# Dense sums computed in PV's 64x32 tiles, on both sides of PV, in a fused attention and gated-MLP kernel

## The chip, the core and the metric

The kernel runs on one core of a Trainium2 chip. A core has one TensorE (PE) for matrix products, three elementwise engines, VectorE (DVE), ScalarE (ACT) and GpSimd (POOL), and SyncE (SP), which here only starts DMA transfers. Each engine works through a queue of its own, strictly in the order in which the program wrote its instructions, and waits at semaphores for what other engines or transfers must deliver. Products are summed in PSUM, eight banks of 128 x 512 float32. The metric is the device time of one execution in microseconds (us).

## The reference

With x of 2048 x 640 (S x D), 32 heads of 20 and a hidden width of 1536:

```python
xn = layernorm(x)                                  # over 640
q, k, v = split(xn @ wqkv)                         # 32 heads, Dh = 20
scores = q k^T * Dh**-0.5, kept where 0 <= i - j < 256
A = softmax(scores) v, heads joined, @ wo
B = (sigmoid(xn @ w_gate) * (xn @ w_up)) @ w_down
out = x + A + B
```

All inputs and the output are bfloat16.

## The kernel before, in words

**Chunks.** The 2048 rows are worked on in four chunks c of 512. For each chunk there are projections to q, k and v, a gate and an up product for each of 12 blocks f of 128 hidden units, attention, and an output stage of four row blocks. Activations lie transposed, as `xnT[c]` (128 x 5 x 512).

**Dense sums.** A "dense sum" is one accumulation of full 128x128 matmuls into one PSUM bank: `pqk` (L330, five matmuls of 512 columns, one for each of five blocks m of q and of k), `pv` (L360, five of 320 columns, for four row blocks s and two halves), `pg` and `pu` (L450, L457, five of 512 columns each), and `y` (12 of 320 columns at L471 over `ht` and `wd`, then five at L478 over `oc` and `wo`; two halves for each row block s). Each is read afterwards by one or two instructions: `st` (L334 on DVE for q, L336 on ACT for k), which SP stores to a scratch in memory; the casts of `pv` into `v` (L369, on DVE for the first half and on ACT for the second); a tanh `th` of `pg` on ACT (L453); `h`, which multiplies `th` and `pu`, on DVE (L461); and `rows` (L482, DVE).

**Attention.** Heads are handled four at a time (a group), two groups at a time (a "head pair" of groups o and o + 1, PSUM accumulators `acc`). The sliding window is cut into squares of 64 x 64, and the squares of a head pair are packed into "score runs" of 128 x 4 x 512 scores: 15 runs for chunk 0 and 20 for each later one, five for each head pair, 75 in all, numbered from 0 in the order of the loop at L754. In a run `scores` (L519) issues matmuls in tiles of 20x64 (20 of the array's rows, 64 of its columns; L526), eight of which work side by side, into `ps`, which takes four PSUM banks; there is one such buffer. One exp on ACT (L531) turns it into a P tile `pT`; POOL then zeroes what the window excludes (`affine_select`, L538). Some steps ("late") get one more mask on DVE (L543, "the edge step"); in chunks 1 to 3 it is the last of a head pair's five runs.

**PV.** When all runs of a head pair are there, `pv` (L545) multiplies P with V in tiles of 64x32 (L557), again eight side by side, into two `acc` banks: 96 matmuls for a head pair. `finish_group` transposes each `acc` on DVE (L569) and puts the scaling (`scale_group`: reciprocal L577, multiplications L581, transpose L585) on the list `fill.behind`, of which one entry goes out with each later piece of dense work, two if `hurry` is set.

**PSUM.** `ps` holds four banks, the pool `ps_d` the other four. Dense sums and the `acc` banks share `ps_d`; a new tile takes the bank that has been free for longest, and its first matmul waits until that bank's last reader is done.

**The order of the work.** The program's order is written by hand. The loop at L754 goes over the 75 runs. If `due` has a head pair at step t, its PV goes out first (run t is then the first run of the next head pair), then run t's scores, and then dense work out of `Fill`: generators that issue a dense sum and yield its cost in ns. `pull` (L623) draws from the front generator until the given ns are used up; `one` (L604) draws once. A step draws 1800 ns (`APART`) and a `credit` that spreads what must be done by a deadline over the steps up to it; a "late" step draws 1000 of it before its edge step. `mix` (L632) puts pieces of a second generator between those of a first: the layer norm of the next chunk (`g_norms`: statistics, then four `xn` on DVE, L291, stored by SP; `g_turns`: transposes to `xnT`, L313), and gate and up sums between v and output sums. The generators in order: gate and up sums of chunk 0, then, for each later chunk, its q and k sums (`g_qk`), its v sums (`g_v`, mixed with gate and up), the rest of its gate and up, and the output of the chunk before it (`g_out`). `shut` holds an output stage back until the last PV of its chunk.

**Q and K.** The stores of `st` are read back by `spread` (L340) into `qT` and `kT` tiles of two head pairs (128 x 4 x 512), from pools `qp` (3) and `kp` (5). A zeroed tile of the `kT` pool clears the padding of the scratch at the start (L194).

Of the kernel before, what the change touches and what calls it, by code (L numbers as in the profile page):

```python
# [9 lines left out]
P = 128  # L10
S = 2048
D = 640
H = 32
DH = 20
F = 1536
DC = D // P
FC = F // P
CW = 512
NCH = S // CW
SBC = CW // P  # L20
HG = 4
NG = H // HG
GH = NG // 2
VW = DH + 1
VH = 16 * VW + 11
HALF = 320
# [12 lines left out]
BF16 = mybir.dt.bfloat16  # L39
FP32 = mybir.dt.float32  # L40
# [6 lines left out]
U = 64  # L47
PTW = 10 * U
# [64 lines left out]
def kernel(  # L113
# [11 lines left out]
    nc = tc.nc  # L125
# [4 lines left out]
    def pool(name, bufs, **kw):  # L130
        return ctx.enter_context(tc.tile_pool(name=name, bufs=bufs, **kw))
# [3 lines left out]
    lnp = pool("lnp", 4)  # L135
    xtp = pool("xtp", 2)
    stp = pool("stp", 6)
    qp = pool("qp", 3)
    kp = pool("kp", 5)
    vp = pool("vp", 10)  # L140
    hp = pool("hp", 15)
    pp = pool("pp", 5)
    op = pool("op", 7)
    onp = pool("onp", 2)
    tp = pool("tp", 2)
# [19 lines left out]
    wd = const.tile([P, FC, D], BF16, name="wd")  # L165
# [24 lines left out]

    scratch = {w: tc.dram_tile([H * 32, CW], BF16, name=f"s{w}") for w in "qk"}
    xn_rows = [tc.dram_tile([CW, D], BF16, name=f"xr{k}") for k in range(2)]
    zero = kp.tile([P, GH, CW], BF16, name="kT")
    nc.gpsimd.memset(zero[:, 0:3, :], 0.0)  # L194

    def clear(w):
        rows = scratch[w].rearrange("(h j) s -> h (j s)", j=32)[:, DH * CW:]
        nc.sync.dma_start(out=rows.rearrange("h (a e) -> h a e", a=4), in_=zero[:, 0:3, :])

    def load_gu(t, w, k, lo=0, hi=FS):  # L200
        nc.sync.dma_start(out=t[k][:, :, lo:hi],
# [118 lines left out]
    qk = {}  # L320
    vt = {}

    def proj_block(w, c, m):


        base = 0 if w == "q" else D
        ps = ps_d.tile([P, CW], FP32, name="pqk", tag="d")
        for d in range(DC):
            wt = wqkv[:, d, base:base + D].rearrange("p (k m) -> p m k", m=DC)
            nc.tensor.matmul(ps, lhsT=wt[:, m, :], rhs=xnT[c][:, d, :],  # L330
                             start=(d == 0), stop=(d == DC - 1))
        st = stp.tile([P, CW], BF16, name="st")
        if w == "q":
            nc.vector.tensor_copy(out=st, in_=ps)  # L334
        else:
            nc.scalar.copy(out=st, in_=ps)  # L336
        dst = scratch[w].rearrange("(h j) s -> h j s", j=32)
        nc.sync.dma_start(out=dst[:, 4 * m:4 * m + 4, :], in_=st)

    def spread(w, c, g0, g1):  # L340

        half, first = divmod(g0, GH)
        if first == 0:
            qk[w, c, half] = (qp if w == "q" else kp).tile([P, GH, CW], BF16, name=w + "T")
        src = scratch[w].rearrange("(a b p) s -> b p a s", a=2, p=P)
        for b in range(g0 // 2, g1 // 2):
            o = 2 * b - half * GH
            nc.sync.dma_start(out=qk[w, c, half][:, o:o + 2, :], in_=src[b])

    def new_v(c, s):  # L350
        v = vp.tile([P, 2, VH], BF16, name="v")
# [1 line left out]
        nc.gpsimd.memset(v[:, :, 0:16 * VW].rearrange("p k (h d) -> p k h d", d=VW)[:, :, :, DH:VW], 0.5)  # L353
        nc.gpsimd.memset(v[:, :, 16 * VW:], 0.0)

    def project_v(c, s, hf, lo=0, hi=DC, ps=None):
        if ps is None:
            ps = ps_d.tile([P, CW], FP32, name="pv", tag="d")
        for d in range(lo, hi):
            nc.tensor.matmul(ps[:, 0:HALF], lhsT=xnT[c][:, d, s * P:(s + 1) * P],  # L360
                             rhs=wqkv[:, d, 2 * D + hf * HALF:2 * D + (hf + 1) * HALF],
                             start=(d == 0), stop=(d == DC - 1))
        return ps

    def copy_v(c, s, hf, ps, copy, us=(0, 1)):

# [5 lines left out]
    def proj_v(c, s, hf, copy):  # L372
        copy_v(c, s, hf, project_v(c, s, hf), copy)
# [29 lines left out]
            yield 0  # L403

    def g_qk(c):
        for w in "qk":
            for m in range(DC):
                proj_block(w, c, m)
                if c == 0 and w == "q" and m == 1:
                    load_x(1)  # L410
                if c == 0 and w == "q" and m == 3:
                    load_gu(wu, B_w_up, 0, FS // 2)
                if c and w == "k" and m == 1:
                    spread("q", c, 0, GH)
                yield 5 * MM
        if c == 0:
            spread("q", c, 0, 2)
            spread("k", c, 0, 2)
            spread("q", c, 2, 4)
            spread("k", c, 2, 4)  # L420

    def g_v(c):
        for s in range(SBC):
            new_v(c, s)
            for hf in range(2):
                proj_v(c, s, hf, nc.scalar.copy if hf else nc.vector.tensor_copy)
                if hf == 0:
                    yield 5 * 136
            if s == 0:
                spread("k", c, 0, 2)  # L430
                spread("k", c, 2, GH)
            if c == 1 and s == 1:
                load_wo()
            if s == (2 if c == 1 else 1):
                spread("q", c, GH, NG)
                spread("k", c, GH, NG)
            yield 5 * 136


    ht = {}  # L440
# [1 line left out]
    def part(w, d, f):  # L442
        k, first = divmod(f * P, FS)
        return w[k][:, d, first:first + P]

    def g_gu(c, f0, f1):
        for f in range(f0, f1):
            pg = ps_d.tile([P, CW], FP32, name="pg", tag="d")
            for d in range(DC):
                nc.tensor.matmul(pg, lhsT=part(wg, d, f), rhs=xnT[c][:, d, :],  # L450
                                 start=(d == 0), stop=(d == DC - 1))
            th = tp.tile([P, CW], FP32, name="th")
            nc.scalar.activation(out=th, in_=pg, func=TANH, scale=0.5)  # L453
            yield 5 * MM
            pu = ps_d.tile([P, CW], FP32, name="pu", tag="d")
            for d in range(DC):
                nc.tensor.matmul(pu, lhsT=part(wu, d, f), rhs=xnT[c][:, d, :],  # L457
                                 start=(d == 0), stop=(d == DC - 1))
            h = hp.tile([P, CW], BF16, name="h")
            ht[c, f] = h  # L460
            nc.vector.scalar_tensor_tensor(out=h, in0=th, scalar=1.0, in1=pu, op0=ADD, op1=MULT)  # L461
            yield 5 * MM


    oc = {}
# [7 lines left out]
            if f % 6 == 5:  # L473
                yield 6 * 136

    def add_wo(c, s, y, cut):
        for m in range(DC):
            nc.tensor.matmul(y[:, 0:cut[1] - cut[0]], lhsT=oc[c, m][:, s * P:(s + 1) * P],  # L478
                             rhs=wo[:, m, cut[0]:cut[1]], start=False, stop=(m == DC - 1))

    def add_x(y, cut, rows):
        nc.vector.scalar_tensor_tensor(  # L482
# [9 lines left out]
        sb = c * SBC + s  # L492
        queue.dma_start(out=out2[sb * P:(sb + 1) * P, cut[0]:cut[1]], in_=rows[:, cut[0]:cut[1]])

    def outp(c, s, ys, rows):
        for y, cut in zip(ys, HALVES):
            add_wo(c, s, y, cut)
        for y, cut in zip(ys, HALVES):
            add_x(y, cut, rows)
        store(c, s, rows)  # L500

    def g_out(c, between, ahead=()):
        nxt = new_rows(c, 0)
        for s in range(SBC):
            rows = nxt
            if s == 0:
                yield from ahead
            if s + 1 < SBC:
                nxt = new_rows(c, s + 1)
            ys = [ps_d.tile([P, CW], FP32, name=f"y{i}", tag="d") for i in range(2)]  # L510
            for y, cut in zip(ys, HALVES):
                yield from down(c, s, y, cut)
            if s == 0:
                yield from between
            outp(c, s, ys, rows)
            yield 10 * 136


    def scores(c, step):  # L519
        pt = pp.tile([P, HG, PTW], BF16, name="pT")  # L520
        ps = ps_s.tile([P, HG, CW], FP32, name="ps")
        for o, j, q, n, col in sorted(step["pieces"], key=lambda x: -x[3]):
            kc, kb = divmod(c * CW // U + j, CW // U)
            for a in range(2):
                for i in range(HG):
                    nc.tensor.matmul(  # L526
                        ps[a * U:(a + 1) * U, i, col * U:(col + n) * U],
                        lhsT=qk["k", kc, o // GH][32 * i:32 * i + DH, o % GH + a, kb * U:(kb + 1) * U],
                        rhs=qk["q", c, o // GH][32 * i:32 * i + DH, o % GH + a, q * U:(q + n) * U],
                        start=True, stop=True)  # L530
        nc.scalar.activation(out=pt[:, :, 0:CW], in_=ps, func=EXP, scale=SCALE)  # L531
        for diag, u, n in step["masks"]:
# [217 lines left out]
    fill.pull(6 * 5 * MM)  # L750
    parts = {}
    credit = 0
    fill.shut = {"out0", "out1", "out2"}
    for t, (c, k, step) in enumerate(todo):  # L754
        if k == 0 and c > 0:
            fill.until(f"qk{c}")
        if k == 2 and c > 0:
            fill.until(f"v{c}")
        if t in due:
            fill.flush()  # L760
            pair = due[t]
            fill.hurry = pair[1] == NG - 2
            pv(*pair, parts.pop(pair))
            if pair[1] == NG - 2:
                fill.shut.discard(f"out{pair[0]}")
        pt, late = scores(c, step)
        for o, *piece in step["pieces"]:
            parts.setdefault((c, o), []).append((pt, *piece))
        last, label = next(x for x in cuts if t < x[0])
        credit += fill.left(label) / (last - t)  # L770
        rest = APART
        if late:
            rest = APART - FIRST_PART + fill.pull(FIRST_PART)
            late()
        credit -= APART - fill.pull(rest)
        credit = fill.pull(credit)
# [66 lines left out]
```

## Time and profile before

| | us |
|---|---|
| median of 3 runs | 309.19 (308.82 to 309.40) |
| profiled execution, its own time | 309.21 |
| its span | 306.9 |
| PE busy | 303.3 |
| ACT busy | 197.6 |
| DVE busy | 179.3 |
| POOL busy | 164.1 |
| granted TensorE clock, mean | 1.000 |

The span is the time from the first to the last instruction of the profiled execution; its own time has some 2.3 us more. By the view of stretches PE is busy for all of 12 to 296 us, with ACT at 37 of 58 us (12 to 70), 60 of 80 (70 to 150), 55 of 80 (150 to 230) and 37 of 66 (230 to 296). Matmuls are pipelined, so the mean duration of one (380 ns at 512 columns) is a latency; the pace is the time between their starts.

### The profile page before, as it was taken

How to read it: one execution, taken by the hardware profiler on the slowest of the kernel's cores; microseconds unless marked ns; L12 is line 12 of the kernel's file. 1: busy time of each engine (PE TensorE's matmuls, PEld its weight loads, DVE VectorE, ACT ScalarE, POOL GpSimd, SP SyncE). 2: the span in 40 equal slices, each digit the busy share in tenths (PEclk: the TensorE clock that was granted, in tenths of full speed). 3: DMA queues.
4: the chain of work that ended last, by engine and by line, in shares of the span. 5: the costliest groups of instructions: out<-in, count | busy, mean ns of one | idle time of the engine just before them, and what ended most of it. 6: DMA issues, size and time to landing. Idle time of an engine off the chain costs nothing.

```text
span 306.9 us, 10122 instructions
## 1 busy us (share of the span) xinstructions
PE 303.3 (99%) x4376; PEld 171.8 (56%) x4376; DVE 179.3 (58%) x356; ACT 197.6 (64%) x194; POOL 164.1 (53%) x304
## 2 busy tenths in 40 slices
PE   8999999999999999999999999999999999999996
PEld 7654444555657654554557665554546665444774
DVE  4735657889856569683826555482733627362433
ACT  6833768688965648888655538978585547778000
POOL 3020667479883728666472827657382756557000
PEclk9999999999999999999999999999999999999999
DMA  7997969546574152774001112650000200000202
GB/s 209 365 321 241 320 219 277 160 130 183 132 246 116 44 161 73 243 212 87 4 0 47 65 67 84 200 168 2 2 2 2 79 32 23 0 4 0 88 23 64
DMA packets 40147, 36.03 MB, mean 117 GB/s; under 512 B 9000, under 2 KB 39848, under 8 KB 40104
## 3 DMA queue, kind: packets, MB, share of 16 engines
q1 hardware_dynamic: 39240, 34.63, 37.1%
q10 hardware_dynamic: 864, 0.77, 0.9%
q8 instruction: 34, 0.56, 0.8%
q14 instruction: 9, 0.07, 0.1%
HBM read 24.77 MB, written 10.62 MB: 115 GB/s over the span
## 4 chain that ended last, share of the span: by engine, by line
PE 97%; DMA 2%; SPq 0%; DVE 0%; issue 0%
PE y L471 18%; PE pu L457 17%; PE pg L450 17%; PE pqk L330 15%; PE ps L526 9%; PE pv L360 8%; PE y L478 7%; PE acc L557 6%; DMA wqkv<-in_A_wqkv_dram 2%; SPq L176 0%; PE pt L298 0%; DVE xn L482 0%
## 5 line engine op out<-in xcount | busy, mean ns | idle before, releaser
L538 POOL TENSOR_SCALAR_AFFINE_SELECT pT<-pT 64x512 bf16<-64x512 bf16 (+1 forms) x252 | 152.6, 606 | 90.6 <-ACT pT L531 78.9
L531 ACT ACTIVATE pT<-ps 128x2048 bf16<-128x2048 f32 x75 | 140.8, 1877 | 59.0 <-PE ps L526 57.2
L461 DVE SCALAR_TENSOR_TENSOR h<-th,pu 128x512 bf16<-128x512 f32 x48 | 32.7, 684 | 56.9 <-PE pu L457 43.4
L457 PE MATMUL pu<-xnT,wu 128*128 128x512 bf16 x240 | 59.8, 380 | 0.0
L450 PE MATMUL pg<-xnT,wg 128*128 128x512 bf16 x240 | 59.8, 380 | 0.0
L471 PE MATMUL y<-wd,h 128*128 128x320 bf16 (+2 forms) x396 | 56.6, 295 | 0.0
L330 PE MATMUL pqk<-xnT,wqkv 128*128 128x512 bf16 x200 | 46.0, 381 | 0.0
L471 PEld LDWEIGHTS <-h 128*128 128x128 bf16 x396 | 36.7, 98 | 15.9 <-issue 2.2
L453 ACT ACTIVATE th<-pg 128x512 f32<-128x512 f32 x48 | 28.6, 596 | 15.3 <-PE pg L450 15.1
L450 PEld LDWEIGHTS <-wg 128*128 128x128 bf16 x240 | 22.2, 98 | 25.6 <-issue 2.0
L457 PEld LDWEIGHTS <-wu 128*128 128x128 bf16 x240 | 22.1, 98 | 25.4 <-issue 1.8
L330 PEld LDWEIGHTS <-wqkv 128*128 128x128 bf16 x200 | 22.5, 119 | 18.7 <-issue 1.2
L526 PE MATMUL ps<-qT,kT 20*64 20x320 bf16 (+4 forms) x1456 | 31.9, 259 | 0.0
L526 PEld LDWEIGHTS <-kT 20*64 20x64 bf16 x1456 | 15.7, 103 | 24.3 <-issue 21.8
L569 DVE STREAM_TRANSPOSE t<-acc 128x512 f32<-128x512 f32 x32 | 21.1, 694 | 13.7 <-PE acc L557 13.7
L482 DVE SCALAR_TENSOR_TENSOR rows<-y,rows 128x320 bf16<-128x320 f32 x30 | 14.2, 483 | 22.3 <-PE y L478 20.6
L360 PE MATMUL pv<-wqkv,xnT 128*128 128x320 bf16 x160 | 25.8, 300 | 0.0
L478 PE MATMUL y<-wo,oc 128*128 128x320 bf16 (+2 forms) x165 | 24.2, 295 | 0.0
L557 PE MATMUL acc<-pT,v 64*32 64x320 bf16 (+4 forms) x1456 | 19.7, 252 | 0.0
L557 PEld LDWEIGHTS <-v 64*32 64x32 bf16 x1456 | 16.4, 91 | 5.8 <-ACT pT L531 1.2
L360 PEld LDWEIGHTS <-xnT 128*128 128x128 bf16 x160 | 14.6, 98 | 8.6 <-issue 1.3
L478 PEld LDWEIGHTS <-oc 128*128 128x128 bf16 x165 | 15.6, 98 | 6.3 <-issue 0.4
(51 smaller groups left out, 182.9 us busy)
## 6 DMA issues: line engine op xcount, KB each, us to landing
qT<-sq SPq DMA_DIRECT2D x16, 256.0 KB
kT<-sk SPq DMA_DIRECT2D x16, 256.0 KB
sq<-st SPq DMA_DIRECT2D x20, 128.0 KB
sk<-st SPq DMA_DIRECT2D x20, 128.0 KB
out_dram<-rows SPq DMA_DIRECT2D x15, 160.0 KB
wg<-in_B_w_gate_dram SPq DMA_DIRECT2D x4, 480.0 KB
wu<-in_B_w_up_dram SPq DMA_DIRECT2D x4, 480.0 KB
xc<-in_A_x_dram SPq DMA_DIRECT2D x3, 640.0 KB
```

What stands on the lines that cost most here:

```text
L330: nc.tensor.matmul(ps, lhsT=wt[:, m, :], rhs=xnT[c][:, d, :], start=(d == 0), stop=(d == DC - 1))
L360: nc.tensor.matmul(ps[:, 0:HALF], lhsT=xnT[c][:, d, s * P:(s + 1) * P], rhs=wqkv[:, d, 2 * D + hf * HALF:2 * D + (hf + 1) * HALF], start=( ...
L450: nc.tensor.matmul(pg, lhsT=part(wg, d, f), rhs=xnT[c][:, d, :], start=(d == 0), stop=(d == DC - 1))
L453: nc.scalar.activation(out=th, in_=pg, func=TANH, scale=0.5)
L457: nc.tensor.matmul(pu, lhsT=part(wu, d, f), rhs=xnT[c][:, d, :], start=(d == 0), stop=(d == DC - 1))
L461: nc.vector.scalar_tensor_tensor(out=h, in0=th, scalar=1.0, in1=pu, op0=ADD, op1=MULT)
L471: nc.tensor.matmul(y[:, 0:cut[1] - cut[0]], lhsT=ht[c, f][:, s * P:(s + 1) * P], rhs=wd[:, f, cut[0]:cut[1]], start=(f == 0), stop=False)
L478: nc.tensor.matmul(y[:, 0:cut[1] - cut[0]], lhsT=oc[c, m][:, s * P:(s + 1) * P], rhs=wo[:, m, cut[0]:cut[1]], start=False, stop=(m == DC - 1))
L526: nc.tensor.matmul(ps[a * U:(a + 1) * U, i, col * U:(col + n) * U], lhsT=qk["k", kc, o // GH][32 * i:32 * i + DH, o % GH + a, kb * U:(kb + ...
L531: nc.scalar.activation(out=pt[:, :, 0:CW], in_=ps, func=EXP, scale=SCALE)
L538: nc.gpsimd.affine_select(out=view, in_=view, pattern=[[0, HG], [0, n], [sign, U]], compare_op=GE, fill=0.0, base=base, channel_multiplier ...
L557: nc.tensor.matmul(acc[32 * i:32 * i + 32, q * U:(q + n) * U], lhsT=vt[kb][a * U:(a + 1) * U, u, h * VW:h * VW + 32], rhs=pt[a * U:(a + 1) ...
```

## The change

At 15 of the steps at which PV is due (`INSIDE`), PV goes between two dense sums, and those two sums are computed in PV's tile shape. The step issues run t's scores, then the first half of the two sums, PV, and the second half. Before, it issued PV, run t's scores and then dense work.

`two_sums` does it: two dense sums are made at the same time in tiles of 64x32. In its first half the upper 64 rows of the array sum into one bank and the lower 64 into the other, eight tiles side by side; in its second half they swap, so that each sum gets both halves of its 128 terms. Between the halves a DVE copy of one column of the second bank is issued, and then PV (taken from the list `middle`). The two sums are: two q or k blocks (steps 8, 25, 45), both v halves of a row block (12, 30, 50), gate and up of a hidden block (4, 35, 55, 65, 70), or both 12-term down sums of a row block (16, 20, 40, 60). The number in `INSIDE` says how many pieces of dense work are drawn ahead of PV and the scores; these, and the block, are booked against `credit`, and the step draws no other dense work (`continue`). Steps not listed issue PV ahead of the scores as before.

In a block of q or k sums the first goes to `st` on DVE, the second on ACT if it is of k and else on DVE; single sums go as before. In a block both casts or tanh and `h` follow the second half. Q and K tiles hold one head pair (128 x 2 x 512; pools of 5 and 9 in place of 3 and 5), there are six P tiles in place of five, and the zeroed tile is a P tile.

```diff
-    qp = pool("qp", 3)
-    kp = pool("kp", 5)
+    qp = pool("qp", 5)
+    kp = pool("kp", 9)
...
-    pp = pool("pp", 5)
+    pp = pool("pp", 6)
...
-    zero = kp.tile([P, GH, CW], BF16, name="kT")
-    nc.gpsimd.memset(zero[:, 0:3, :], 0.0)
+    zero = pp.tile([P, HG, PTW], BF16, name="pT")
+    nc.gpsimd.memset(zero[:, 0:3, 0:CW], 0.0)
...
+    def one_sum(name, terms, width=CW, stop=True):
+        ps = ps_d.tile([P, CW], FP32, name=name, tag="d")
+        for k, (left, right) in enumerate(terms):
+            nc.tensor.matmul(ps[:, 0:width], lhsT=left, rhs=right, start=(k == 0), stop=stop and k == len(terms) - 1)
+        return ps
+
+    def two_sums(names, terms, width=CW):
+        ps = [ps_d.tile([P, CW], FP32, name=name, tag="d") for name in names]
+        last = len(terms[0]) - 1
+        for turn in range(2):
+            for k in range(last + 1):
+                for a in range(2):
+                    b = a ^ turn
+                    left, right = terms[b][k]
+                    for i in range(HG):
+                        nc.tensor.matmul(ps[b][32 * i:32 * i + 32, 0:width],
+                                         lhsT=left[a * U:(a + 1) * U, 32 * i:32 * i + 32],
+                                         rhs=right[a * U:(a + 1) * U], skip_group_check=True,
+                                         start=(turn == 0 and k == 0), stop=(turn == 1 and k == last))
+            if turn == 0:
+                nc.vector.tensor_copy(out=scr, in_=ps[1][:, 0:1])
+                middle.pop()()
+        return ps
...
-        half, first = divmod(g0, GH)
-        if first == 0:
-            qk[w, c, half] = (qp if w == "q" else kp).tile([P, GH, CW], BF16, name=w + "T")
...
+            qk[w, c, b] = (qp if w == "q" else kp).tile([P, 2, CW], BF16, name=w + "T")
+            nc.sync.dma_start(out=qk[w, c, b], in_=src[b])
...
+            now = [todo.pop(0) for _ in range(2 if middle else 1)]
+            terms = [proj_terms(w, c, m) for w, m in now]
+            pss = two_sums(["pqk"] * 2, terms) if middle else [one_sum("pqk", terms[0])]
+            for k, ((w, m), ps) in enumerate(zip(now, pss)):
+                proj_store(w, m, ps, nc.scalar.copy if w == "k" and k == len(now) - 1 else nc.vector.tensor_copy)
...
-                yield 5 * MM
+            yield len(now) * 5 * MM
+            for _ in now[1:]:
+                yield 0
...
+            both = bool(middle)
+            if both:
+                pss = two_sums(["pv"] * 2, [v_terms(c, s, hf) for hf in range(2)], HALF)
+                for hf, copy in enumerate((nc.vector.tensor_copy, nc.scalar.copy)):
+                    copy_v(c, s, hf, pss[hf], copy)
+                yield 0
...
+            both = bool(middle)
+            pg, pu = two_sums(("pg", "pu"), terms) if both else (one_sum("pg", terms[0]), None)
             th = tp.tile([P, CW], FP32, name="th")
             nc.scalar.activation(out=th, in_=pg, func=TANH, scale=0.5)
-            yield 5 * MM
...
+            if both:
+                yield 0
+            else:
+                yield 5 * MM
+                pu = one_sum("pu", terms[1])
...
-            yield 5 * MM
+            yield (10 if both else 5) * MM
...
+    def down_both(c, s):
+        terms = [[(ht[c, f][:, s * P:(s + 1) * P], wd[:, f, lo:hi]) for f in range(FC)] for lo, hi in HALVES]
+        return two_sums(("y0", "y1"), terms, HALF)
...
+            closed = bool(middle)
+            if closed:
+                ys = down_both(c, s)
+                yield 24 * 136
+                for _ in range(3):
+                    yield 0
...
     credit = 0
+    INSIDE = {4:0,8:0,12:0,16:0,20:1,25:0,30:2,35:1,40:2,45:0,50:1,55:0,60:1,65:1,70:1}
...
+        inside = t in INSIDE
+        if inside:
+            ahead = INSIDE[t]
+            while ahead:
+                cost = fill.one()
+                ahead -= cost > 0
+                credit -= cost
         if t in due:
             fill.flush()
             pair = due[t]
             fill.hurry = pair[1] == NG - 2
-            pv(*pair, parts.pop(pair))
-            if pair[1] == NG - 2:
-                fill.shut.discard(f"out{pair[0]}")
+            middle.append(lambda pair=pair: pv(*pair, parts.pop(pair)))
+            if not inside:
+                middle.pop()()
         pt, late = scores(c, step)
+        while middle:
+            credit -= fill.one()
+        if t in due and pair[1] == NG - 2:
+            fill.shut.discard(f"out{pair[0]}")
...
         credit += fill.left(label) / (last - t)
+        if inside:
+            continue
```

## The prediction

> **What bounds the kernel now.** The page's first part and its chain come first, then the chain around one PV:
>
> ```profile
> PE 303.3 (99%) x4376; PEld 171.8 (56%) x4376; DVE 179.3 (58%) x356; ACT 197.6 (64%) x194; POOL 164.1 (53%) x304
> ...
> q8 instruction: 34, 0.56, 0.8%
> ...
> PE 97%; DMA 2%; SPq 0%; DVE 0%; issue 0%
> ```
>
> PE carries 97% of the chain, and the view of waits has no row in which a matmul of the main loop waits for ACT, DVE or POOL. So a wait that the change brings to PE counts in full. The chain around run 30 (start, us, what):
>
> ```profile
> 126.87 1.08 PE pg L450 x5
> 127.94 0.68 PE pv L360 x5
> 128.62 1.22 PE acc L557 x96
> 129.85 0.36 PE ps L526 x24
> 130.20 1.19 PE pu L457 x5
> ```
>
> Five dense matmuls take 1.08 us at 512 columns (216 ns each) and 0.68 at 320. What is not column time is the switch between tile shapes. The timeline of single engines shows it alone, and shows how little room the single score buffer leaves:
>
> ```profile
> 255.17 0.43 PE L526 MATMUL ps<-qT,kT 20*64 20x320 bf16 x24
> ...
> 255.53 1.25 PE L450 MATMUL pg<-xnT,wg 128*128 128x512 bf16 x5
> ...
> 255.72 1.88 ACT L531 ACTIVATE pT<-ps 128x2048 bf16<-128x2048 f32 x1 [0.68 <-PE ps L526]
> ...
> 276.80 1.24 PE L450 MATMUL pg<-xnT,wg 128*128 128x512 bf16 x5
> ...
> 277.97 0.42 PE L526 MATMUL ps<-qT,kT 20*64 20x320 bf16 x16
> 278.08 0.60 ACT L453 ACTIVATE th<-pg 128x512 f32<-128x512 f32 x1 [0.25 <-PE pg L450]
> ...
> 278.33 1.25 PE L457 MATMUL pu<-xnT,wu 128*128 128x512 bf16 x5
> 278.57 1.87 ACT L531 ACTIVATE pT<-ps 128x2048 bf16<-128x2048 f32 x1
> ```
>
> From pg to the scores: 277.97 - 276.80 - 1.08 = 0.09 us for a switch. Scores start to exp's end: 257.60 - 255.17 = 2.43 and 280.44 - 277.97 = 2.47. A run's scores take 0.36 with the switch behind them (278.33 - 277.97), so the next run can start without a wait only if about 2.1 us of other PE work lies between. Two 512-wide sums (2.16, 2.35 with both switches) just do. Durations on the queues that may now be late, from the groups by shape (busy us, mean ns of one):
>
> ```profile
> L461 DVE SCALAR_TENSOR_TENSOR h<-th,pu 128x512 bf16<-128x512 f32 x48 | 32.7, 684 | 56.9 <-PE pu L457 43.4 <-ACT th L453 13.3
> ...
> L450 PEld LDWEIGHTS <-wg 128*128 128x128 bf16 x240 | 22.2, 98 | 25.6 <-issue 2.0
> ...
> L369 DVE CAST v<-pv 64x320 bf16<-64x320 f32 x31 | 15.1, 486 | 5.9 <-PE pv L360 5.6
> ...
> L369 ACT CAST v<-pv 64x320 bf16<-64x320 f32 x33 | 13.9, 421 | 1.4 <-PE pv L360 0.6
> ...
> L585 DVE STREAM_TRANSPOSE oc<-on 128x512 bf16<-128x512 bf16 x16 | 11.4, 711 | 0.6
> L336 ACT CAST st<-pqk 128x512 bf16<-128x512 f32 x20 | 11.2, 597 | 8.2 <-PE pqk L330 8.2
> L581 DVE TENSOR_TENSOR on<-t,rec 128x320 bf16<-128x320 f32 x16 | 10.4, 651 | 0.6
> ...
> L291 DVE TENSOR_SCALAR xn<-xc,mvs,rstds 128x640 bf16<-128x640 bf16 x12 | 6.9, 593 | 0.0
> L543 DVE TENSOR_TENSOR pT<-pT,edge 128x512 bf16<-128x512 bf16 x15 | 6.6, 441 | 13.0 <-ACT pT L531 12.5
> ```
>
> **The change part by part.** Base: the profiled execution, 309.21 us (span 306.9 and 2.3 around it), 0.02 from the median of 309.19. "Run t" is the t-th score run, "block" two sums with PV inside.
>
> *Switches.* In the program orders PE changes tile shape 167 times before and 150 after. 17 x 0.09 = **-1.6**. Scores to 64x32 tiles is not in the trace; the four kinds that are cost 0.09 to 0.10, so I price it the same (ends: 0 and 0.2 for each of 15, -1.4 to +1.6).
>
> *Dense sums as tiles.* 206 matmuls become 1648, eight side by side. PV in that shape: 20480 columns over eight are 2560, 1.07 us at the 2.4 columns per ns that 512 in 0.216 give; the chain has 1.22 with a switch, so its loads hide. Price **0**, PV being the nearest row, of the same shape. The ends: upward, one exposed load of 91 ns (16.4 us over PV's 1456) for each group of eight, 206 x 0.091 = 18.7, with rival 4 as the milder form; below nothing, a group that is quicker than a full-array matmul (rival 3). Both ends are cases of their own below.
>
> *Runs 66 and 67.* The order has run 67 straight behind run 66, no dense matmul between: the block at run 65 books the cost of its gate and up sums late, and that booking uses up the next step's share. One score buffer, so run 67 waits for exp 66, 2.43 to 2.47 after run 66 started instead of 0.27, plus the signal: **+2.3** (2.2 to 2.4).
>
> *Run 30's block.* PV's second accumulator takes the bank of the up sum before it, which is read by h. On DVE in front of h now stand, in this order, the edge step (behind exp 29), one xn, two casts, three xn. From run 29's start PE needs: scores and switch 0.36, pu, pv, pg, pv, pu 4.60, switch, run 30 and switch 0.45, first half of the block 0.68: 6.1. ACT: three k copies and tanh and two casts stand around exp 28, so exp 29 ends about 2.9 to 3.1 after run 29's start; then 0.44 + 4 x 0.59 + 2 x 0.49 + 0.68 = 4.5, less up to 0.5 where neighbours overlap: 6.9 to 7.6. **+1.1** (0.8 to 1.7).
>
> *out1's first down sum.* After the block at run 35 come pg, pu, six y, run 37, six y; the last of these reads the h of that pu. From the block's end PE is there after 4.6. On DVE before that h: an h that waits for tanh (0.8 + 0.7), then the scaling of two groups with two transposes (3.0 to 3.6), then 0.68: 5.2 to 5.8. **+0.9** (0.6 to 1.5).
>
> *Run 12's block.* Its accumulators take the banks of two k sums, which ACT copies (0.6 each) after exp 11, and exp 12 stands behind the copies: PV 0.15 late, run 13 0.3 late. **+0.4** (0.3 to 0.8).
>
> *Run 15 to 16.* Only pv and pu between (1.76 and switches). ACT before exp 15: exp 14, two casts, a tanh. Exp 15 ends 5.7 after run 14 started, PE is there at 5.1. **+0.6** (0.4 to 0.8).
>
> *Run 31 to 32; 58 to 59.* In the first, exp 31 stands behind two casts of the block (0.84); in the second only pu and six y (1.90) lie between. **+0.5** (0.4 to 0.6).
>
> *xnT of chunk 1.* In the trace its last transpose ends 0.2 us before the first q sum. PV at run 4 moves 1.5 us later on PE and everything behind it on DVE; idle spots of DVE (0.8, 0.5, 0.4) take up most. **+0.4** (0 to 1.3).
>
> *At nothing.* The 15 copies of one column (some 0.16 each by DVE's 128x1 reciprocals) hold DVE until the first half ends; the accumulator transposes behind them wait for PV anyway, and the second half, which waits for the copy, has PV's 1.1 us as cover; gone, it costs 0.4 each. The next sum takes an accumulator's bank, free 0.9 after PV, while the half and scores need 1.2: nothing, 0.2 each if DVE is late. A P tile now lives one run longer, which the sixth covers. Q and K per pair: same loads, same place in SP's queue, freed earlier; the tile of zeros goes out in pieces of 1 KB before SP idles from 12.1 to 15.4 us. POOL keeps its list, and PV starts later than its masks. Ends for these together: -0.3 to +1.
>
> Sum: -1.6 + 2.3 + 1.1 + 0.9 + 0.4 + 0.6 + 0.5 + 0.4 = +4.6, so 309.2 + 4.6 = **313.8 us**. With every wait at its low or high end: +3.1 and +7.5 (waits of 4.7 and 9.1).
>
> **The rivals.**
>
> 1. *The queues catch up.* DVE and ACT are 58% and 64% busy; if neighbours overlap wherever they can, only run 67's wait stays: -1.6 + 2.3 = +0.7, 309.9. Against: the two chains of run 30 and out1 miss by more than the overlap.
>
> 2. *PE runs short of instructions.* The change adds 2884 to 8754. The trace has 34 fetches, 0.56 MB, so 16 KB or 256 instructions each, 1.2 us of one engine (0.8% of 16 x 306.9 over 34). Before, 256 PE instructions never took under 2.5 us; in a block they take 1.6 to 2.0. If a fetch with its start takes 2.0 us or more and only one is kept ahead, each of the 15 blocks waits 0.2 to 0.5: +3 to +7, and 313.8 + 5 = 318.8. No such wait shows before. [...]
>
> 3. *Faster: groups of eight beat full-array matmuls.* If the halves of the array overlap so that a group takes less than the matmul it replaces, 206 groups gain; the sum turns faster from 4.6 / 206 = 22 ns a group. At twice that, 206 x 0.044 = 9.1 and 313.8 - 9.1 = 304.7. Against: PV's 1.22 us leaves no room below its column time.
>
> 4. *Weight loads set the pace.* A 128x128 load is busy for 98 ns; if a quarter of its columns took a quarter, 24.5 ns, and eight came one behind the other, a group would need 0.196: nothing at 512 columns (0.216), 0.060 more at 320 (0.136). The v and y blocks have 3 x 10 + 4 x 24 = 126 such groups: +7.6, 321.4. Against: PV's twelve groups of eight, most under 320 columns, took 1.22 and not 12 x 0.196 = 2.35. [...]
>
> **How the numbers follow.** Forecast (several waits, 312.3 to 316.7): 0.62. Rival 1 (309.3 to 312.3): 0.13. Rival 2 (316.7 to 321): 0.12. Rival 4: 0.03. Rival 3 and anything else that is faster: 0.10. The range 309.3 to 318.6 leaves out rivals 3 and 4 and half of rival 2, 0.19 together. A measurement of this kernel can tell about 0.2% (0.6 us) from no change; the low edge of rival 1 lies within that, so 0.05 for the same and 0.85 for slower.
>
> **What would show it.** After: an idle PE of some 2.3 us between two score runs near 265 us, with exp as the releaser; matmuls of acc and y released by h on DVE, near 135 and 160 us; TensorE's groups of eight 216 ns apart at 512 columns; scores to tiles 0.09. Wrong if groups of eight differ from 216 or 136 ns, if PE idles inside blocks with nothing late (instructions), or if DVE's chains end before PE asks.

## The result and the profile after

| us | before | after |
|---|---|---|
| median of 4 runs each | 309.14 (308.82 to 309.40) | 334.33 (331.57 to 340.70) |
| profiled execution, its own time | 309.21 | 331.57 |
| its span | 306.9 | 329.7 |
| its mean granted clock | 1.000 | 1.000 |

The ratio of the times is 1.0786 (95% interval 1.0720 to 1.0851; the slow execution of 340.70, at a mean granted clock of 0.980, is not in it): slower by some 24 us. The forecast was 313.8, the range ended at 318.6. The profiled execution is the fastest of the four; two of the others have a mean granted clock of 0.989 to 0.990 and 334.2 and 334.5 us, and the last part of this document comes to why.

The page of the changed kernel: the engines (first part), the fetches of instructions (third part) and the chain that ended last:

```profile
PE 305.9 (93%) x5818; PEld 176.0 (53%) x5818; DVE 179.9 (55%) x371; ACT 197.7 (60%) x194; POOL 163.0 (49%) x304
...
q8 instruction: 45, 0.74, 1.0%
...
PE 83%; issue 6%; ACT 5%; DVE 5%; DMA 1%; SPq 0%; DVEq 0%; ACTq 0%
```

PE was 99% busy and is 93% busy. The chain, 97% PE before, now has three entries that were at or near nothing: 5% each of ACT and DVE (their whole instructions, not only PE's idle time behind them), and 6% "issue", time in which PE waited for nothing that the profile shows. There are 45 fetches of instructions in place of 34.

The view of waits, PE's matmuls alone (what waited, for what, us in total, times, longest):

```profile
PE y L343 <- issue: 5.5, 3, 2.3
PE acc L599 <- issue: 2.9, 3, 1.3
PE ps L568 <- ACT pT L573: 2.4, 2, 2.1
PE pg L343 <- issue: 2.0, 2, 1.5
PE ps L568 <- issue: 1.8, 2, 1.3
PE pqk L343 <- issue: 1.6, 1, 1.6
PE pv L343 <- issue: 0.9, 1, 0.9
...
PE y L502 <- DVE h L492: 0.8, 1, 0.8
PE acc L599 <- DVE h L492: 0.7, 1, 0.7
```

L343 are the dense sums in tiles, L599 is PV, L568 the scores. Before, this view had no such row for the main loop. The rows with a named releaser (exp `pT`, `h`) are those that the prediction listed. The rows with "issue" are new and larger.

One block, step 16, in the timeline of PE (start, us, what, idle before):

```profile
85.64 0.43 PE L568 MATMUL ps<-qT,kT 20*64 20x320 bf16 x24 [0.29 <-ACT pT L573]
85.99 1.95 PE L343 MATMUL y<-wd,h 64*32 64x320 bf16 x96
87.65 1.12 PE L599 MATMUL acc<-pT,v 64*32 64x320 bf16 x72
88.55 0.72 PE L343 MATMUL y<-wd,h 64*32 64x320 bf16 x27
91.60 1.41 PE L343 MATMUL y<-wd,h 64*32 64x320 bf16 x69 [2.33 <-issue]
92.93 0.42 PE L568 MATMUL ps<-qT,kT 20*64 20x320 bf16 x16
```

The second half of the two y sums stops in its middle, after 27 of 96 matmuls, for 2.5 us and then runs on. Nothing in the program stands at that place: no wait, no other operand. The records of the instruction queue (q8) have a fetch that starts at 89.10, the moment at which the matmuls stop.

Where the 22.4 us went, from the records of single matmuls in the profiled execution (idle counted from the end of a matmul's columns to the next start, without the 0.09 of a change of shape):

| | us |
|---|---|
| 14 stops with no releaser, all in blocks or right behind them, 0.27 to 2.49 each | +17.7 |
| 7 waits for exp, `h`, a cast of `v`, `xnT` | +5.5 |
| 17 changes of shape fewer, 0.09 each | -1.6 |
| not assigned | +0.8 |

### The profile page after: what moved, and what is told of

It reads as the page before. It is cut to its first block, busy times and chain, and to the rows that moved or that the text cites. A ratio compares the mean times of both kernels' runs of the same rounds, so it can differ in the third digit from the quotient of the medians.

```text
span 329.7 us, 13037 instructions
## 1 busy us (share of the span) xinstructions
PE 305.9 (93%) x5818; PEld 176.0 (53%) x5818; DVE 179.9 (55%) x371; ACT 197.7 (60%) x194; POOL 163.0 (49%) x304
## 4 chain that ended last, share of the span: by engine, by line
PE 83%; issue 6%; ACT 5%; DVE 5%; DMA 1%; SPq 0%; DVEq 0%; ACTq 0%
PE pg L329 13%; PE pu L329 12%; PE y L502 12%; PE pqk L329 12%; PE ps L568 7%; PE y L513 7%; PE acc L599 5%; PE pv L329 5%; PE y L343 4%; ACT pT L573 3%; PE pqk L343 2%; PE pg L343 2%; PE pu L343 1%; PE pv L343 1%; DVE h L492 1%
## 5 line engine op out<-in xcount | busy, mean ns | idle before, releaser
L329 PE MATMUL pg<-xnT,wg 128*128 128x512 bf16 x215 | 53.6, 380 | 0.0
L329 PE MATMUL pu<-xnT,wu 128*128 128x512 bf16 x215 | 53.5, 380 | 0.0
L502 PE MATMUL y<-wd,h 128*128 128x320 bf16 (+2 forms) x300 | 42.7, 294 | 0.9 <-DVE h L492 0.8
L329 PE MATMUL pqk<-xnT,wqkv 128*128 128x512 bf16 x170 | 39.1, 381 | 0.3 <-DVE xnT L313 0.3
L568 PE MATMUL ps<-qT,kT 20*64 20x320 bf16 (+4 forms) x1456 | 32.4, 259 | 4.3 <-ACT pT L573 2.4
L502 PEld LDWEIGHTS <-h 128*128 128x128 bf16 x300 | 27.9, 98 | 13.5 <-issue 2.0
L568 PEld LDWEIGHTS <-kT 20*64 20x64 bf16 x1456 | 15.9, 103 | 31.5 <-issue 31.1
L329 PEld LDWEIGHTS <-wu 128*128 128x128 bf16 x215 | 20.1, 98 | 23.6 <-issue 1.8
L329 PEld LDWEIGHTS <-wg 128*128 128x128 bf16 x215 | 19.6, 98 | 22.7 <-issue 1.8
L329 PEld LDWEIGHTS <-wqkv 128*128 128x128 bf16 x170 | 19.2, 119 | 16.4 <-issue 1.0
L599 PE MATMUL acc<-pT,v 64*32 64x320 bf16 (+4 forms) x1456 | 20.6, 251 | 3.6 <-issue 2.9
L599 PEld LDWEIGHTS <-v 64*32 64x32 bf16 x1456 | 18.1, 91 | 6.8 <-issue 3.7
L329 PE MATMUL pv<-wqkv,xnT 128*128 128x320 bf16 x130 | 21.3, 300 | 0.2 <-DVE v L389 0.2
L343 PE MATMUL y<-wd,h 64*32 64x320 bf16 x768 | 15.6, 297 | 5.5 <-issue 5.5
```

What stands on the lines that cost most here:

```text
L329: nc.tensor.matmul(ps[:, 0:width], lhsT=left, rhs=right, start=(k == 0), stop=stop and k == len(terms) - 1)
L343: nc.tensor.matmul(ps[b][32 * i:32 * i + 32, 0:width], lhsT=left[a * U:(a + 1) * U, 32 * i:32 * i + 32], rhs=right[a * U:(a + 1) * U], ski ...
L502: nc.tensor.matmul(y[:, 0:cut[1] - cut[0]], lhsT=ht[c, f][:, s * P:(s + 1) * P], rhs=wd[:, f, cut[0]:cut[1]], start=(f == 0), stop=False)
L568: nc.tensor.matmul(ps[a * U:(a + 1) * U, i, col * U:(col + n) * U], lhsT=qk["k", kc, o // 2][32 * i:32 * i + DH, a, kb * U:(kb + 1) * U], ...
L599: nc.tensor.matmul(acc[32 * i:32 * i + 32, q * U:(q + n) * U], lhsT=vt[kb][a * U:(a + 1) * U, u, h * VW:h * VW + 32], rhs=pt[a * U:(a + 1) ...
```

## The experiments

Theory A: PE runs out of instructions. They come in pages of 256 (16 KB a fetch; 45 fetches for 5818 matmuls and 5818 weight loads); a page used up faster than the next arrives ends in a stop. B: the new order makes DVE and ACT late everywhere, and what has no releaser is the same lateness. C: dense sums in tiles are themselves slow. D: each added instruction costs its share, wherever it stands. E, which came later: the stops belong to places of the work.

The changed kernel already speaks against C: inside a block the starts of two groups of eight stand 216 ns apart at 512 columns (median of 512 pairs) and 136 at 320 (896 pairs), the full-array figures.

### The blocks as full-array sums

```diff
-        for turn in range(2):
...
+        for b in range(2):
+            for k, (left, right) in enumerate(terms[b]):
+                nc.tensor.matmul(ps[b][:, 0:width], lhsT=left, rhs=right, start=(k == 0), stop=(k == last))
+            if b == 0:
+                nc.vector.tensor_copy(out=scr, in_=ps[0][:, 0:1])
+                middle.pop()()
```

> The changed kernel with its whole order, PV between two sums included, but with the two sums as full 128x128 matmuls again: 8754 PE instructions instead of 11638. Theory A (PE runs short of instructions: a page of 256 that is used up in under some 3.2 us ends in a wait for the next): the stalls inside the blocks, 17.7 us in the changed kernel's trace, go; the 5.5 us of waits for exp, h and xnT stay; PE changes shape 180 times against 167 before, 13 x 0.094 = 1.2. So 309.2 + 5.5 + 1.2 = 315.9, between 314.5 and 317.5. Theory B (the order costs it, the queues of DVE and ACT being late everywhere): stays near 331.

315.6 (313.96 to 315.94), ratio 1.0201 (1.0172 to 1.0230). The first part of its page:

```profile
PE 306.4 (98%) x4376; PEld 170.5 (54%) x4376; DVE 180.1 (57%) x371; ACT 197.7 (63%) x194; POOL 162.9 (52%) x304
```

PE is back at 98%. Of PE's waits in the main loop, the view of waits has one above 0.5 us, scores for exp:

```profile
PE ps L561 <- ACT pT L566: 2.6, 3, 2.1
```

Its longest is that of run 67, in PE's timeline:

```profile
260.51 0.43 PE L561 MATMUL ps<-qT,kT 20*64 20x320 bf16 x24
263.06 0.42 PE L561 MATMUL ps<-qT,kT 20*64 20x320 bf16 x16 [2.13 <-ACT pT L566]
```

All 17.7 us of stops without a releaser are gone and the order is the same, so B is out as the main cause. Run 67 still waits 2.3 us for exp 66. The rest of the lateness is 1.5 us here (0.49, 0.34, 0.29, 0.24, 0.17) and not 3.2, partly because this version isn't a pure undo: its one-column copy reads the other sum's bank, and at run 30 PV does not wait for `h`: its matmuls start at 132.38 us, that `h` at 132.56. That the banks rotate differently is argued, not shown. At full clock the sum closes: 309.0 (before, measured beside it) + 13 x 0.094 + 3.8 = 314.0, and the one execution at a mean clock of 1.000 took 313.96.

### More instructions, spread evenly

The kernel before with the 512-wide matmuls halved (the gate sum shown):

```diff
-                nc.tensor.matmul(pg, lhsT=part(wg, d, f), rhs=xnT[c][:, d, :],
-                                 start=(d == 0), stop=(d == DC - 1))
+                for lo in (0, 256):
+                    nc.tensor.matmul(pg[:, lo:lo + 256], lhsT=part(wg, d, f), rhs=xnT[c][:, d, lo:lo + 256],
+                                     start=(d == 0 and lo == 0), stop=(d == DC - 1 and lo == 256), skip_group_check=True)
```

> The kernel before, its order untouched, with every 512-wide matmul of the q, k, gate and up sums split into two of 256 columns: 10114 PE instructions instead of 8754, spread evenly and not in bursts, about 20 in 1.08 us. Theory A: a page of 256 still lasts over 3.2 us nearly everywhere, so 309 to 311. Theory D (each added instruction costs its share wherever it stands, 22.4 us over the change's 2884 being 7.8 ns): 1360 x 7.8 ns = 10.6, so 319.8.

312.25 (311.88 to 314.84), ratio 1.0125 (1.0076 to 1.0175): 3.3 us, where D asked for 10.6. It is above A's range too, in part for a reason that is not A's: a 256-wide matmul starts 109 ns after the one before it and not 108, so the 680 added matmuls cost some 2 ns each, 1.4 us. Another 1.4 is one stop, A's own, in an order that had none; a wait of 0.3 for a load of `kT` is most of the rest. PE's timeline:

```profile
200.11 1.29 PE L560 MATMUL acc<-pT,v 64*32 64x320 bf16 x96
201.33 0.43 PE L529 MATMUL ps<-qT,kT 20*64 20x320 bf16 x24
...
204.65 0.37 PE L529 MATMUL ps<-qT,kT 20*64 20x320 bf16 x9
206.30 0.29 PE L529 MATMUL ps<-qT,kT 20*64 20x128 bf16 x15 [1.27 <-issue]
```

A score run, two steps behind a PV, stops after nine of its 24 matmuls. The kernel before was not far from this: it came to its closest page 3.0 us after that page's fetch had started, where the stops of the changed kernel end 2.3 to 2.5 us after it in most cases.

### PV issued twice, and four times

```diff
+        flat = flat + flat
         for k, (pt, j, q, n, col) in enumerate(flat):
```

> The kernel before with every PV's matmuls issued twice in a row into the same sums (numerators and denominators double): no dense sum in tiles, no new order, 11666 PE instructions, 384 of them in each PV. Columns: 16 x 1.07 = 17.1 us more, 326.3 if nothing else costs. Theory A: a PV now uses a page of 256 in about 1.5 us, so that 11 of the 16 meet a page that is not there yet, 0.2 to 1.9 us each, 17.0 together: 343.3, between 340 and 347. Theory C (tiles are only slow in dense sums, by their 512 columns or their two banks): 326.

352.43 (348.89 to 353.07), ratio 1.138 (1.1322 to 1.1437). With no dense tile and no new order in it, 26 us more than its columns ask for. The profiled execution has eleven stops of 0.3 to 3.8 us (and two of 0.2) that end 2.2 to 3.0 us after the start of a fetch; C is out. My price was low by 9 us: the stops are 20.7 together, the longest 3.4 and 3.8 where I had at most 1.9, and three stretches at half clock follow (below).

Four times, to see the pace of the fetches alone (`flat = flat * 4`):

> The kernel before with every PV's matmuls issued four times in a row into the same sums (numerators and denominators times four): 768 PE instructions in each PV, three pages of 256 on end, so that the pace of fetching itself shows. Columns: 16 x 3 x 1.07 = 51.4 us more, 360.6 if nothing else costs. Theory A: within a PV the starts of two fetches stand 3.2 to 3.5 us apart and a page's matmuls take no less than that, for 1.5 us of columns: some 68 us of stalls, 425 to 432, more (up to 455) if the stalls bring stretches at half clock. Theory C: 361.

438.39 (437.12 and 439.67), ratio 1.418. The page:

```profile
PE 366.6 (84%) x8709; PEld 224.1 (51%) x8744; DVE 177.9 (41%) x356; ACT 197.5 (45%) x194; POOL 163.8 (37%) x304
...
q8 instruction: 68, 1.11, 1.1%
...
PE 83%; issue 15%; DMA 1%; ACT 0%; DVE 0%; SPq 0%
```

15% of the chain is "issue". Within a PV the starts of successive fetches are mostly 3.3 to 4.0 us apart (185.19 and 188.74 in one, 205.31, 208.83, 212.75 and 216.03 in and behind another), and a page's 128 matmuls have 1.4 us of columns. That is the pace: 256 instructions in 3.3 to 4.0 us.

### Half the instructions in the same columns

```diff
-                    for i in range(HG):
-                        nc.tensor.matmul(ps[b][32 * i:32 * i + 32, 0:width],
-                                         lhsT=left[a * U:(a + 1) * U, 32 * i:32 * i + 32],
+                    for i in range(2):
+                        nc.tensor.matmul(ps[b][64 * i:64 * i + 64, 0:width],
+                                         lhsT=left[a * U:(a + 1) * U, 64 * i:64 * i + 64],
```

> The changed kernel with the two sums of a block in tiles of 64x64, four side by side, instead of 64x32: the same columns in half the matmuls, 9990 PE instructions. Theory A: 4.5 to 6.9 us of stalls instead of 17.7; 180 changes of shape instead of 150, if one between 64x64 and 64x32 costs as much as the others. 309.2 + 5.5 + 1.2 + 5.5 = 321.4, between 319 and 324; 2.8 less if the changes between the two tile shapes are free. Theory B: near 331.

321.21 (320.33 to 322.60), ratio 1.0397 (1.0364 to 1.0430), the time that A said. Stops without a releaser: five, 3.5 us, in place of 14 and 17.7. That is less than the 4.5 to 6.9 expected, so that the time came out within 0.2 us is in part luck: the profiled execution also has a stretch at half clock (mean 0.995), and the two at 1.000 took 320.3 and 320.7. The changes between 64x64 and 64x32 are not free: 0.093 each, like the others.

### The same work, 100 instructions later

```diff
-            pss = two_sums(["pqk"] * 2, terms) if middle else [one_sum("pqk", terms[0])]
+            pss = two_sums(["pqk"] * 2, terms) if middle else [(halved if c == 0 else one_sum)("pqk", terms[0])]
```

> The changed kernel with each of chunk 0's ten q and k sums, long before the first block, as ten matmuls of 256 columns instead of five of 512: 100 PE instructions more ahead of all blocks, nothing else. In the changed kernel's trace each stall inside a block ends at an instruction whose number in PE's program is 176 to 213 above a multiple of 256. Theory A (pages of 256): the stalls stay at those numbers and so move by 100 instructions of the work, to other matmuls: blocks that had none get one and the other way round; their sum stays at 16 to 21 us (17.7 before the shift), the time between 330 and 336. Theory E (the stalls belong to places of the work, a bank or a late reader): they stay at the same matmuls.

The stops sum to 18.9 us (13 of them), as A said. The time, 339.08 (337.79 to 342.76), is above my 330 to 336; its mean granted clock is 0.975 to 0.989 in all four executions. The profiled one has three stretches at half clock, by the 1.7 us each that the last part finds some 5 us of its 338.6. The place of each stop decides between A and E. The number is that of the instruction at which PE goes on, counted in PE's program:

| instruction | of 256 | changed kernel: us, what | shifted: us, what |
|---|---|---|---|
| 2746 | 186 | 2.49, y in tiles | 1.72, PV |
| 3510 | 182 | 1.45, PV | 0.99, PV |
| 3766 | 182 | 0.83, y full array | 1.51, y in tiles |
| 6576 | 176 | 1.64, y in tiles | 2.23, y in tiles |
| 7344 | 176 | 1.41, scores | 1.11, q or k in tiles |
| 9388 | 172 | 1.82, y in tiles | 1.03, PV |
| 9644 | 172 | 0.27, y full array | 1.73, y in tiles |
| 10922 | 170 | 0.69, scores | 1.01, up sum in tiles |
| 1152, shifted 1252 | | 0.48, waits for `xnT` | 0.99, the same |
| 2308, shifted 2408 | | 0.37, waits for exp | 0.65, the same |
| 4784, shifted 4884 | | 0.88, waits for `h` | 0.88, the same |
| 5834, shifted 5934 | | 0.98, waits for `h` | 0.96, the same |

The waits for other engines move with the work, by exactly 100. The stops keep their numbers and so fall on other matmuls; those that are in one kernel only keep the spacing as well (all 27 of the two kernels are at 170 to 190 of 256, and so are those of the split, the doubled, the 64x64 and the two other versions with blocks). The slow drift from 190 to 170 is the count's: it leaves out some 25 instructions for semaphores that PE's trace has too. Counted with them, every one of these stops, in all seven kernels, is at 192 or 193 of 256. E is out, and A is shown as directly as the records allow: it is the page that stops PE.

The block of step 35 shows it. In the changed kernel it ran without a stop; shifted, its last matmul comes 0.7 us late, in PE's timeline:

```profile
159.95 0.39 PE L351 MATMUL pu<-xnT,wu 64*32 64x512 bf16 x4
159.96 0.38 PE L351 MATMUL pg<-xnT,wg 64*32 64x512 bf16 x3
160.87 0.39 PE L351 MATMUL pg<-xnT,wg 64*32 64x512 bf16 x1 [0.53 <-issue]
```

Three of four tiles that work side by side have started, and the fourth is, by that count, the first instruction of a page.

### Three smaller ones

Full-array sums, and a gate and up block booked in one piece:

```diff
-            if both:
-                yield 0
-            else:
+            if not both:
                 yield 5 * MM
                 pu = one_sum("pu", terms[1])
```

> The version with full-array sums around PV, and the block of a gate and up sum booked in one piece, without the draw of cost 0 between, so that the step after it draws its share: dense work comes between runs 66 and 67. The wait of 2.3 us for exp 66 goes, and with it the stretch at half clock that followed it in three of four executions (1.7 us, 315.8 against 313.96). So 313.96 - 2.3 = 311.7, between 310.8 and 312.6, the granted clock 1.000. If the drop of the clock has nothing to do with that wait, it stays in some executions, at 0.995 and 313.4.

314.61 (313.85 to 315.38), ratio 1.0181 (1.0156 to 1.0205), above my 310.8 to 312.6. The wait of run 67 is gone, as expected. But a wait for `xnT` of 2.5 us has come at 54.6 us, one for exp of 1.4 at 212.6, and one stop of 1.0 at the end of a page. The draw of cost 0 was also a place at which a piece of the layer norm went out; that its loss makes `xnT` late is argued, not shown. And the clock fell in one of four executions (0.995) without the wait that I held for its only cause; the new wait of 2.5 us is as long.

The change without its blocks (`INSIDE = {}`):

> The changed kernel with an empty list of block steps: PV where it was before, all sums full 128x128, and of the change only the six P tiles, Q and K tiles of one pair and the zeroed P tile. No wait is known that these would move: 309.0, between 308.5 and 309.6. If the pools carry part of the loss, it shows here.

308.53 (308.14 to 308.86, ten runs), ratio 0.9988 (0.9979 to 0.9997). The pools and tiles carry nothing of the loss. It is the fastest of all versions here, by 0.12%, less than the 0.2% that I take for certain.

Only four gate and up blocks, in tiles, booked in one piece (`INSIDE = {35: 1, 55: 0, 65: 1, 70: 1}`):

> The changed kernel with blocks only at steps 35, 55, 65 and 70, where the two sums are gate and up (512 columns, 160 instructions for 2.16 us), booked in one piece. 165 changes of shape, 0.2 us less than before. Theory A: a block with its PV and scores still uses 352 instructions and more in 3.6 us, and each meets a page that is late by 0.5 to 1.25: 2 to 5 us, some 0.5 for out1's first h: 311.5 to 314.5. If a block of 512 columns gets by with the page in hand: 309.0 to 309.6.

313.12 (313.01 to 313.43), ratio 1.0137 (1.0122 to 1.0152). Three of the four blocks meet the end of a page, 0.9 to 1.1 us each. The gain of a block is one change of shape, 0.09 us. In tiles, sums of 512 columns have the fewest instructions per us of all the dense sums here (160 in 2.16 us), so by this run none of them is long enough to pay.

## Why the prediction was wrong

- **What bounds the kernel: right.** PE had no slack, and every wait counted in full.
- **Switches: right.** 17 fewer; scores to 64x32 tiles, which the trace of before did not show, took 0.091.
- **Dense sums as tiles at nothing: right for the arithmetic, wrong for the price.** Groups of eight run at 216 and 136 ns, so rivals 3 and 4 are both out. What a group costs is its 16 instructions against two. One reading in that step was off: the 91 ns are the row's mean duration of one load, not 16.4 us over 1456, which is 11 ns; it moved only the upper end, which the 216 and 136 ns rule out.
- **The waits: right, and they were the forecast.** Predicted 6.2 us, measured 5.5 in the profiled execution: run 67 2.3 (2.29), run 30 1.1 (0.88), out1's first y 0.9 (0.98), run 15 to 16 0.6 (0.37), `xnT` 0.4 (0.48), 31 to 32 and 58 to 59 0.5 (0.17, the second alone), run 12 0.4 (none there; 0.29 before a v sum two runs on). Taken by themselves they and the switches give 313.1. Single terms missed by up to 0.4, and the 5.5 were measured in an order that also stops 14 times, in which DVE and ACT can catch up; how long they would be without the stops is not shown (the version with full-array sums had 3.8).
- **The step that failed is rival 2, its price and its chance.** In the sum, waits for instructions stood at nothing; they measured 17.7 us, nearly four times the +4.6 that the sum added. I had the mechanism, the page of 256, the one page kept ahead and the rate in a block (1.6 to 2.0 us a page), and gave it 0.12 and 3 to 7 us. Its price hung on "a fetch with its start takes 2.0 us or more", and nothing bounded that from above: the only row was the transfer itself, 1.2 us. In the changed kernel matmuls go on 2.3 to 2.5 us after the transfer starts in most stops, and the start itself mostly comes 0.4 to 1.9 us after PE has entered the page before. End to end that was 3.5 and 4.0 us for the two pages between two stops, and 3.3 to 4.0 with PV issued four times. Against 1.6 to 2.0 us of work, a page boundary in a block then costs 1.3 us in the mean of the 14 that stop (17.7 / 14), not 0.2 to 0.5.
- **What misled me** was that before, 256 instructions never took less than 2.5 us and no wait showed. I read that as proof that a fetch is faster than 2.5 us. It only said that no single page, with its boundaries where they happened to lie, was used up before the next had come; with 1360 instructions more the same order stopped once.
- **How far ahead the pages come.** The trace has one page in use and one ahead: in the changed kernel, over its 45 fetches, that of a page starts between 2.0 us before and 3.7 us after PE's first matmul of the page before it, never several pages early. Nor is fetching hidden there: the 14 stops are 17.7 us together, where matmuls are small.

## What to carry to other kernels

Eight small tiles side by side have the columns of one large matmul and eight times its instructions; count the instructions of a stretch as well as its columns, and hold 256 of them against the 3.3 to 4.0 us that they took here with PV issued four times. A change that saves 0.09 us at a place must not put hundreds of instructions more there, and a stop in the middle of a loop, with "issue" as its releaser and the same place modulo 256 in the program, was here each time a page that had not come. Where the trace shows only the transfer of a resource and not the time until it can be used, the bound from above is open, and the range has to say so.

## What the runs showed that I had not expected

**An idle PE can cost twice.** In the version with full-array sums PE stood still for 2.3 us behind run 66, and from 264.7 to 268.3 us each 512-wide matmul took 0.43 us and not 0.216. The view of stretches (start and end, length, busy time of PE, PEld, DVE, ACT, POOL, granted clock, busy share of DMA, GB/s):

```profile
263.00:264.70 1.70, 1.64 (x22) 0.76 (x22) 0.88 (x2) 1.16 (x2) 1.52 (x3) 0.97 0.05 10
264.70:268.30 3.60, 3.60 (x25) 1.05 (x24) 0.69 (x1) 2.02 (x3) 3.33 (x6) 0.54 0.00 0
268.30:280.00 11.70, 11.70 (x203) 5.58 (x202) 5.08 (x10) 7.68 (x8) 4.94 (x9) 1.00 0.01 1
```

The granted clock is 0.54 in that stretch. Executions with it (mean 0.995) took 315.4 to 315.9, the one without 313.96: 1.7 us for one stretch. Such stretches would account for the spread of the changed kernel's own times, 331.57 at 1.000, 334.2 and 334.5 at 0.989 and 0.990; of those only the first has a trace.

To see what brings it, 14 pauses of PE were put into the kernel before:

```diff
+        if t in PAUSES:
+            pause(PAUSES[t])
...
+    def pause(n):
+        w = ps_d.tile([P, CW], FP32, name="pz", tag="d")
+        nc.tensor.matmul(w[:, 0:P], lhsT=ident, rhs=ident, start=True, stop=True)
+        held = lnp.tile([P, P], BF16, name="held", bufs=2)
+        nc.vector.tensor_copy(out=held, in_=w[:, 0:P])
+        for _ in range(n):
+            nxt = lnp.tile([P, P], BF16, name="held", bufs=2)
+            nc.vector.tensor_copy(out=nxt, in_=held)
+            held = nxt
+        nc.tensor.matmul(w[:, 0:P], lhsT=held, rhs=ident, start=True, stop=True)
```

> The kernel before with 14 pauses of PE: at the end of 14 steps a matmul of 128 columns that waits for a chain of 2 to 13 copies on DVE behind another such matmul, so that PE stands still for some 1 to 4 us by turns. Only the profile counts. Theory F (an idle PE of 2 us and more can bring a stretch of about 3.6 us at half clock, 1.7 us more on top of the wait): after pauses under 1.5 us none, after some of those of 2 to 3 us, after nearly all over 3 us. Theory G (the drop has nothing to do with how long PE stood still): it comes after short ones as often, or away from the pauses.

Idle of PE in us, and whether a stretch at half clock followed: 1.06 no, 1.38 no, 2.08 no, 2.11 no, 2.20 yes, 2.47 yes, 2.62 no, 2.99 yes, and 3.08, 3.65, 3.77, 3.83, 4.31, 4.82 yes. Theory F holds: none under 2, all from 3, some between. By the trace's records of the granted clock three of the nine stretches last 3.41 us and six 6.83, twice that, and a stretch can begin inside the pause. Their starts (77.34, 118.30, 142.19, 162.67, 186.57, 230.94, 275.31, 316.27 and 340.17 us) stand 12, 7, 6, 7, 13, 13, 12 and 7 times 3.413 us apart: they lie on one fixed grid. Here are two pauses in stretches cut on this grid, of 2.47 us (336.49 to 338.96, yes) and of 2.62 us (294.25 to 296.87, no):

```profile
336.75:340.17 3.42, 1.21 (x21) 0.60 (x22) 2.05 (x4) 1.04 (x2) 1.94 (x4) 1.00 0.00 0
340.17:343.58 3.41, 3.41 (x10) 1.21 (x9) 0.69 (x1) 1.58 (x2) 1.83 (x4) 0.50 0.00 0
343.58:346.99 3.41, 3.25 (x30) 1.41 (x30) 0.77 (x2) 2.33 (x3) 0.41 (x1) 1.00 0.00 0
292.38:295.79 3.41, 2.03 (x16) 1.28 (x14) 1.24 (x4) 1.46 (x1) 2.23 (x5) 1.00 0.31 96
295.79:299.21 3.42, 2.34 (x31) 1.58 (x32) 1.07 (x4) 1.68 (x1) 0.52 (x1) 1.00 0.01 2
299.21:302.62 3.41, 3.41 (x46) 2.04 (x52) 1.29 (x3) 2.07 (x2) 2.24 (x4) 1.00 0.14 48
```

The shorter pause falls with 2.2 us into one window of the grid, and the next window runs at half clock; the longer one is shared by two windows, 1.5 and 1.1 us, and nothing follows. So it goes through the trace: the nine windows at full clock in which PE stood idle for 2.19 us or more are each followed by one at half clock, and no window with 2.04 or less is. A window of 3.41 us need not be idle throughout for this: 2.19 us of it were enough. In the version with full-array sums 1.9 us in one window was enough, so what exactly counts as idle stays open near 2 us. In the changed kernel's profiled execution, counted on the grid of its one record at half clock, behind the last matmul, the stop of 2.5 us and the wait of 2.3 were both shared by two windows, with at most 1.8 us of idle in any: by that count, its full clock was luck.
